# Denominator of a rational activation summed in PSUM by diagonal matmuls, with a new instruction order

## The chip, the cores and the metric

The kernel runs on one core of one Trainium2 chip. The metric is the device time of one execution in microseconds; smaller is better. The core's engines run side by side, each taking its own instructions in program order: PE (TensorE, matmuls), DVE (VectorE), ACT (ScalarE), POOL (GpSimd) and SP (here it only issues transfers). Matmuls write to PSUM, a memory of eight banks of 2 KB in each of 128 partitions; PE cannot read from it, ACT and DVE can.

## What is computed

A gated linear attention over 4 batches, 8 heads, 768 tokens and 48 columns a head, then a feed-forward block whose activation is a rational function, 384 to 2048 to 384 columns on 3072 tokens:

```python
f = 1.0 / (1.0 + np.exp(-f_logit))
for t in range(S):
    state = f[:, :, t, :, None] * state + np.einsum('bhd,bhe->bhde', k[:, :, t], v[:, :, t])
    y[:, :, t] = np.einsum('bhd,bhde->bhe', q[:, :, t], state)
...
h = x @ w_in
h2 = h * h
h3 = h2 * h
P = a[0] + a[1] * h + a[2] * h2 + a[3] * h3
Q = 1.0 + np.abs(b[0]) * np.abs(h) + np.abs(b[1]) * h2
g = P / (Q + 1e-06)
return (g @ w_out).astype(np.float32)
```

`x` is the attention's output, `a` has four numbers and `b` two.

## The kernel before

**Attention.** The 768 tokens are cut into six chunks of 128. A unit is one chunk of two batches, so there are twelve units (`NUN`), numbered by chunk and then batch pair. For a unit, `a_ef` makes log(1+exp(-f)) on ACT (an Exp and a Ln), `a_cs` sums it over the tokens by a matmul, `a_exp` takes two exponentials (tiles `A`, `Ai`), `a_mul` multiplies q and k by them on DVE into `qkp`. `a_T` transposes by sixteen matmuls into PSUM (`tp`), `a_Te` copies that to SBUF (`qkT`) on ACT. `a_sc` computes the scores of one batch in PSUM (`sc`), `a_mask` multiplies them by a triangular mask on DVE (`scm`). `a_sv` computes the new state, `a_al` the decay factor on ACT, `a_st` their product on DVE. `a_y` adds what comes from the state and from the scores (`y`), `a_ye` copies it out on ACT (`ysb`), `a_x` transposes it (`xps`) and `a_xe` copies it to `xT`, the input of the ff block, on ACT.

**Feed-forward.** The 2048 ff columns are 16 tiles of 128. A group `n` is four of them for one chunk's 512 tokens, so there are 24 groups (`NGR`), four a chunk, each on tiles of 128 x 2048 elements. `m_h` computes half a group (two ff tiles, three matmuls each) into the two banks of `hp`; `m_y` copies it to bf16 (`hy`) on ACT. On DVE, `m_q` makes z = |h|, w = (|b1| z + |b0|) z, and on ACT `m_ln` takes Ln(w + 1 + 1e-6) and `m_ex` its Exp with scale -1, the reciprocal of Q (`qi`). `m_p` builds the numerator by Horner's rule in five DVE instructions (`t`), and `m_g` multiplies it by `qi` into `gall`. `m_o` computes an output block of 128 tokens from a finished chunk with 16 matmuls, `m_oe` copies it out and SP stores it.

**Order.** The program is under a manual schedule: each engine executes its instructions in the order in which the code emits them. A prologue runs units 0, 1 and most of 2 and starts group 0. The loop then takes two groups and one attention unit per iteration `p`, while `m_o` writes out the chunk before. PSUM's eight banks are pools of one buffer each: `psA` (two banks: scores of the first batch, y), `psB` (two: cs, tp, scores of the second batch), `psh` (two: hp), `ps1` (one: state, xps) and `pso` (one: output). A buffer can be written again when its readers are done, so with one buffer for `hp` each half of a group waits for the copy of the half before. In the last chunk, whose blocks have no later groups to ride along with, `m_o` runs four tiles at a time into `psA` and `psB`.

**Loads.** SP issues in program order q, k and f of a unit (six transfers), the weights and the stores; POOL issues v and converts the weights to bf16. Staging tiles `wst` for the weights have two buffers, the inputs of a unit three.

Of the kernel before, what the change touches and what calls it, by code (L numbers as in the profile page):

```python
# [17 lines left out]
def kernel(  # L18
# [234 lines left out]
    def m_h(n, half):  # L253
        if n >= NGR:
            return
# [1 line left out]
        hp = psh.tile([P, 2, NT], F32, name="hp", tag="h")
# [59 lines left out]
    def m_o(c, b, mms=None):  # L317
        if c < 0:
            return
        if mms is None or mms[0] == 0:  # L320
            if c < NC - 1:
                ops[c, b] = pso.tile([P, DM], F32, name="op")
            else:
                pool = (psA, psB)[b // 2]
                if b % 2 == 0:
                    ops["pair", b // 2] = pool.tile([P, 2, 512], F32, name="op2", tag="AB"[b // 2])
                ops[c, b] = ops["pair", b // 2][:, b % 2, 0:DM]
        for mm in (mms or range(KF)):
# [41 lines left out]
    for g in range(1, NG):  # L370
        load_w_in(g)

    a_ef(0)
    a_cs(0)
    a_exp(0)
    a_mul(0)
# [151 lines left out]
```

## Times and profile before

| | us |
|---|---|
| median of three runs | 312.45 |
| lowest and highest run | 310.96, 314.13 |
| the profiled execution, as timed | 310.16 |
| its span, first to last instruction | 307.8 |
| DVE busy | 267.3 (87%) |
| ACT busy | 224.6 (73%) |
| PE busy with matmuls | 202.7 (66%) |
| POOL busy | 36.4 (12%) |
| mean granted clock of PE, share of full speed | 0.917 |

The profile is of one execution. A busy time is the sum over an engine's instructions, without those that only issue transfers or wait. Ends of matmuls are modelled, and overlap with the next one's start. The granted clock is 1.00 when PE runs at 2.4 GHz and 0.50 at 1.2 GHz; a value between is a mix over the stretch.

### The profile page before, as it was taken

To read this page: it belongs to the slowest core of one execution; us is meant where nothing else is said; L and a number is where in the kernel's file an instruction comes from. 1 tells how busy PE (TensorE), PEld (TensorE's weight loads), DVE (VectorE), ACT (ScalarE), POOL (GpSimd) and SP (SyncE) were. 2 spreads that over 40 slices of the span, in tenths; PEclk is the share of its full clock that TensorE was granted. 3 is DMA by queue.
4 is the path that set the end of the run, shared out by engine and by line. 5 is a ranking of instruction groups with operands and counts; after the bars stand their busy time and mean duration, and the time that the engine had idled before them with its cause. 6 is when DMAs were issued, how large, how long until landed. Compare 5 with 4: busy or idle time off the path is not lost.

```text
span 307.8 us, 4394 instructions
## 1 busy us (share of the span) xinstructions
PE 202.7 (66%) x1752; PEld 110.9 (36%) x1752; DVE 267.3 (87%) x282; ACT 224.6 (73%) x214; POOL 36.4 (12%) x42
## 2 busy tenths in 40 slices
PE   1255673653658686785984976876796758778772
PEld 0234241322324343342542533433443433334331
DVE  3253529999999999999999999999999999999981
ACT  3365477687697699698798697977996886666651
POOL 6012462036002002011020020000000000000000
PEclk9999998679689799799799899998997998999988
DMA  9999699979934009309129019000000000000002
GB/s 137 176 214 232 213 179 160 186 261 258 171 48 26 27 2 173 57 28 160 46 49 159 26 45 186 2 28 26 0 28 26 26 2 26 26 29 26 26 26 102
DMA packets 107315, 27.80 MB, mean 90 GB/s; under 512 B 100640, under 2 KB 105760, under 8 KB 107296
## 3 DMA queue, kind: packets, MB, share of 16 engines
q1 hardware_dynamic: 82336, 25.18, 40.7%
q0 software_dynamic: 24960, 2.36, 14.5%
q8 instruction: 13, 0.21, 0.3%
q14 instruction: 6, 0.05, 0.1%
HBM read 25.17 MB, written 4.72 MB: 97 GB/s over the span
## 4 chain that ended last, share of the span: by engine, by line
DVE 63%; issue 11%; DMA 9%; PE 6%; ACT 5%; SPq 5%; DVEq 0%; ACTq 0%
DVE gall L312 9%; DVE t L303 7%; DVE t L301 7%; DVE w L281 6%; DVE w L282 6%; SPq L97 5%; DVE scm L187 5%; DVE t L300 5%; DVE t L302 4%; DVE z L279 4%; DMA qn<-in_q_dram 4%; DVE qkp L128 3%; DVE t L304 3%; PE op L329 3%; DMA fn<-in_f_logit_dram 2%
## 5 line engine op out<-in xcount | busy, mean ns | idle before, releaser
L262 PE MATMUL hp<-xT,w_in_sb 128*128 128x512 bf16 x288 | 84.1, 435 | 59.3 <-ACT hy L272 57.7
L272 ACT CAST hy<-hp 128x1024 bf16<-128x1024 f32 x48 | 48.2, 1004 | 33.4 <-PE hp L262 33.4
L329 PE MATMUL op<-w_out_sb,gall 128*128 128x384 bf16 x384 | 67.9, 332 | 3.9 <-DVE gall L312 3.9
L262 PEld LDWEIGHTS <-w_in_sb 128*128 128x128 bf16 x288 | 30.3, 106 | 100.0 <-issue 79.9
L288 ACT ACTIVATE lq<-w,one_eps 128x2048 f32<-128x2048 bf16 x24 | 48.2, 2007 | 8.2 <-DVE w L282 8.1
L329 PEld LDWEIGHTS <-gall 128*128 128x128 bf16 x384 | 36.9, 99 | 29.6 <-DVE gall L312 5.3
L293 ACT ACTIVATE qi<-lq 128x2048 bf16<-128x2048 f32 x24 | 45.9, 1911 | 0.8
L187 DVE TENSOR_TENSOR scm<-sc,mask 128x1024 bf16<-128x1024 f32 x24 | 28.2, 1217 | 16.4 <-PE sc L178 16.4
L97 POOL DMA_DIRECT2D vn<-in_v_dram x24 | 22.9, 962 | 101.7 <-PE y L198 100.9
L282 DVE TENSOR_TENSOR w<-w,z 128x2048 bf16<-128x2048 bf16 x24 | 30.7, 1279 | 0.8
L312 DVE TENSOR_TENSOR gall<-t,qi 128x2048 bf16<-128x2048 bf16 x24 | 30.4, 1268 | 0.7
L303 DVE TENSOR_TENSOR t<-t,hy 128x2048 bf16<-128x2048 bf16 x24 | 29.4, 1226 | 0.8
L301 DVE TENSOR_TENSOR t<-t,hy 128x2048 bf16<-128x2048 bf16 x24 | 29.4, 1225 | 0.8
L144 ACT COPY qkT<-tp 128x2048 bf16<-128x2048 bf16 x12 | 22.4, 1866 | 2.3 <-PE tp L136 2.1
L136 PE MATMUL tp<-ident,qkp 128*128 128x128 bf16 x192 | 18.2, 265 | 7.9 <-DVE qkp L127 6.1
L136 PEld LDWEIGHTS <-qkp 128*128 128x128 bf16 x192 | 16.6, 124 | 14.1 <-DVE qkp L127 6.9
L281 DVE TENSOR_SCALAR w<-z,babs 128x2048 bf16<-128x2048 bf16 x24 | 20.1, 839 | 0.9
L300 DVE TENSOR_SCALAR t<-hy,a_sb 128x2048 bf16<-128x2048 bf16 x24 | 20.4, 851 | 0.0
L247 ACT COPY xT<-xps 128x768 bf16<-128x768 bf16 x12 | 9.6, 803 | 14.7 <-PE xps L239 14.7
L127 DVE TENSOR_TENSOR qkp<-qn,A 128x768 bf16<-128x768 f32 x12 | 11.4, 952 | 9.9 <-DMA qn<-in_q_dram 8.2
L304 DVE TENSOR_SCALAR t<-t,a_sb 128x2048 bf16<-128x2048 bf16 x24 | 18.1, 754 | 0.8
L302 DVE TENSOR_SCALAR t<-t,a_sb 128x2048 bf16<-128x2048 bf16 x24 | 18.1, 753 | 0.8
(45 smaller groups left out, 191.6 us busy)
## 6 DMA issues: line engine op xcount, KB each, us to landing
fn<-in_f_logit_dram SPq DMA_DIRECT2D x24, 192.0 KB, 5.2
kn<-in_k_dram SPq DMA_DIRECT2D x24, 192.0 KB, 5.7
qn<-in_q_dram SPq DMA_DIRECT2D x24, 192.0 KB, 5.0
out_dram<-osb SPq DMA_DIRECT2D x24, 192.0 KB, 1.9
wst<-in_moe_w_in_dram SPq DMA_DIRECT2D x4, 768.0 KB, 6.6
wst<-in_moe_w_out_dram SPq DMA_DIRECT2D x4, 768.0 KB, 5.4
vn<-in_v_dram POOLq DMA_DIRECT2D x24, 96.0 KB, 5.6
a_sb<-in_moe_a_dram SPq DMA_DIRECT2D x1, 2.0 KB, 3.7
```

Source lines behind the costliest of these rows:

```text
L97: eng.dma_start(out=dst[:, j], in_=src[u * UB + j, :, t0:t0 + C, :].rearrange("h t d -> t h d"))
L187: nc.vector.tensor_mul(m, s["sc", j].rearrange("s i p t -> s (i p) t"), mb)
L262: nc.tensor.matmul(hp[:, e, :], w_in_sb[:, kk, m * P:(m + 1) * P], xT[:, kk, :], start=(kk == 0), stop=(kk == KD - 1))
L272: nc.scalar.copy(s["y"][:, half * 2 * NT:(half + 1) * 2 * NT], s["hp", half].rearrange("p a n -> p (a n)"))
L281: nc.vector.tensor_scalar(w, z, babs[:, 1:2], babs[:, 0:1], op0=ALU.mult, op1=ALU.add)
L282: nc.vector.tensor_mul(w, w, z)
L288: nc.scalar.activation(s["lq"], s["w"], AF.Ln, bias=one_eps)
L293: nc.scalar.activation(s["qi"], s["lq"], AF.Exp, scale=-1.0)
L301: nc.vector.tensor_mul(t, t, y)
L303: nc.vector.tensor_mul(t, t, y)
L312: nc.vector.tensor_mul(galls[c][:, g * G:(g + 1) * G, :].rearrange("p a n -> p (a n)"), s["t"], s["qi"])
L329: nc.tensor.matmul(ops[c, b], galls[c][:, mm, b * C:(b + 1) * C], w_out_sb[:, mm, :], start=(mm == 0), stop=(mm == KF - 1))
```

## The change

The coefficients are rewritten so that the denominator's two are powers of two times one common factor. `coefficients` splits |b0| and |b1| into a mantissa (`bm`) and a power of two (`bp`). The weights `w_in` are multiplied by m1/m0 while POOL converts them, so h is scaled; the numerator's coefficients take the inverse powers, and the Ln of the denominator takes the factor m0*m0/m1 as its scale (`sig`). The two powers of two stand on the diagonals of two 128 x 128 bf16 matrices (`dg`). For a half group `m_u` multiplies h*h (`h2`, on DVE by `m_sq`) and |h| (`z`, by `m_abs`) by them in PE and adds both in PSUM (`u`), from which `m_ln` reads, 1024 columns at a time. h*h also serves the numerator, which is now (a3 h + a2) h2 + (a1 h + a0): `m_p1`, `m_p2`, `m_p3`. In the last chunk the groups with odd numbers keep their denominator on DVE (`m_w`, `m_lnw`).

PSUM is divided anew: a ring `psr` of two buffers of two banks takes hp, u, cs and in the prologue the second scores; `psA` takes y, tp and both scores, one after the other. The order is rewritten: the prologue has matmuls on zeros (`busy`) between its steps, the ff group's first DVE instructions are ahead of the unit's products, a step of the loop is one group, odd and even steps differ, and the denominator of a group is summed one step after its h (`gp_ = n - 1`). In the last chunk each group's output matmuls follow a step later.

```diff
-    psB = ctx.enter_context(tc.tile_pool(name="psB", bufs=1, space=PSUM))
-    psh = ctx.enter_context(tc.tile_pool(name="psh", bufs=1, space=PSUM))
+    psr = ctx.enter_context(tc.tile_pool(name="psr", bufs=2, space=PSUM))
...
-    def m_q(n):
-
-        s = mg[n]
-        z = ms.tile([P, W], BF16, name="z", bufs=1)
-        nc.vector.tensor_scalar(z.bitcast(U16), s["y"].bitcast(U16), 0x7FFF, None, op0=ALU.bitwise_and)
-        w = ms.tile([P, W], BF16, name="w", bufs=1)
-        nc.vector.tensor_scalar(w, z, babs[:, 1:2], babs[:, 0:1], op0=ALU.mult, op1=ALU.add)
-        nc.vector.tensor_mul(w, w, z)
-        s["w"] = w
...
+    def m_sq(n):
+        s = mg[n]
+        s["h2"] = ms.tile([P, W], BF16, name="h2")
+        nc.vector.tensor_mul(s["h2"], s["y"], s["y"])
+
+    def m_abs(n):
+        s = mg[n]
+        s["z"] = ms.tile([P, W], BF16, name="z")
+        nc.vector.tensor_scalar(s["z"].bitcast(U16), s["y"].bitcast(U16), 0x7FFF, None,
+                                op0=ALU.bitwise_and)
+
+    def m_u(n, half):
+
+        s = mg[n]
+        u = psr.tile([P, 2, NT], F32, name="u", tag="r")
+        for i, src in enumerate((s["h2"], s["z"])):
+            for e in range(2):
+                nc.tensor.matmul(u[:, e, :], dg[:, 1 - i, :],
+                                 src[:, (half * 2 + e) * NT:(half * 2 + e + 1) * NT],
+                                 start=(i == 0), stop=(i == 1))
+        s["u", half] = u
+
+    def m_w(n):
+
+        s = mg[n]
+        s["w"] = ms.tile([P, W], BF16, name="pb", bufs=1)
+        nc.vector.tensor_scalar(s["w"], s["z"], bp[:, 1:2], bp[:, 0:1], op0=ALU.mult, op1=ALU.add)
+        s["u"] = ms.tile([P, W], BF16, name="w", bufs=1)
+        nc.vector.tensor_mul(s["u"], s["w"], s["z"])
+
+    def m_lnw(n):
         s = mg[n]
         s["lq"] = ms.tile([P, W], F32, name="lq", bufs=1)
-        nc.scalar.activation(s["lq"], s["w"], AF.Ln, bias=one_eps)
+        nc.scalar.activation(s["lq"], s["u"], AF.Ln, scale=sig[:, 2:3], bias=1.0 + 1e-6)
+
+    def m_ln(n, half):
+        s = mg[n]
+        if half == 0:
+            s["lq"] = ms.tile([P, W], F32, name="lq", bufs=1)
+        nc.scalar.activation(s["lq"][:, half * 2 * NT:(half + 1) * 2 * NT],
+                             s["u", half].rearrange("p a n -> p (a n)"), AF.Ln,
+                             scale=sig[:, 2:3], bias=1.0 + 1e-6)
...
+    def m_p1(n):
+
+        s = mg[n]
+        s["t"] = ms.tile([P, W], BF16, name="t")
+        nc.vector.tensor_scalar(s["t"], s["y"], a_sb[:, 3:4], a_sb[:, 2:3], op0=ALU.mult, op1=ALU.add)
+        nc.vector.tensor_mul(s["t"], s["t"], s["h2"])
+
+    def m_p2(n):
+        s = mg[n]
+        s["pb"] = ms.tile([P, W], BF16, name="pb", bufs=1)
+        nc.vector.tensor_scalar(s["pb"], s["y"], a_sb[:, 1:2], a_sb[:, 0:1], op0=ALU.mult, op1=ALU.add)
+
+    def m_p3(n):
+        s = mg[n]
+        nc.vector.tensor_add(s["t"], s["t"], s["pb"])
...
-        nc.gpsimd.tensor_copy(w_in_sb[:, :, g * G * P:(g + 1) * G * P], t)
+        nc.gpsimd.tensor_scalar(w_in_sb[:, :, g * G * P:(g + 1) * G * P], t, sig[:, 0:1], None, op0=ALU.mult)
...
+    def busy(k):
+
+        for _ in range(k):
+            nc.tensor.matmul(warm, zeros[:, 0:P], zeros, start=True, stop=True)
...
+        nc.vector.reciprocal(rm, bm)
+        nc.vector.tensor_mul(sig[:, 0:1], bm[:, 1:2], rm[:, 0:1])
+        nc.vector.tensor_mul(sig[:, 1:2], bm[:, 0:1], rm[:, 1:2])
+        nc.vector.tensor_mul(sig[:, 2:3], bm[:, 0:1], sig[:, 1:2])
+        for i in range(3):
+            nc.vector.tensor_scalar(a_sb[:, 1 + i:4], a_sb[:, 1 + i:4], sig[:, 1:2], None, op0=ALU.mult)
+        for i in range(2):
+            nc.vector.tensor_scalar(dg[:, i, :], ident, bp[:, i:i + 1], None, op0=ALU.mult)
...
+    m_h(0, 0)
+    m_h(0, 1)
+    m_y(0, 0)
+    m_y(0, 1)
+    a_ef(2)
+    m_h(1, 0)
+    m_y(1, 0)
+    a_cs(2)
+    m_h(1, 1)
+    a_exp(2, 0)
+    a_exp(2, 1)
+    m_y(1, 1)
+    busy(5)
...
+    for n in range(1, NGR - NG):
+        gp_, gn, gh = n - 1, n, n + 1
+        if n % 2:
+            mu, mf = (n + 5) // 2, (n + 3) // 2
...
+    for n in range(NGR - NG, NGR):
+        g = n % NG
+        if n % 2:
+            m_w(n)
+            m_lnw(n)
...
+    for b in range(B):
+        m_o(NC - 1, b, range((NG - 1) * G, NG * G))
         m_oe(NC - 1, b, (nc.scalar, nc.vector)[b % 2])
```

What the order does is seen in the engines' instructions. On DVE, in the middle of the loop, a group that carries the masks stood so before (z, w and t are the group's tiles, `scm` the masked scores, `gall` the product with the reciprocal):

```order
L279 TENSOR_SCALAR z<-hy 128x2048
L281 TENSOR_SCALAR w<-z,babs 128x2048
L282 TENSOR_TENSOR w<-w,z 128x2048
L300 TENSOR_SCALAR t<-hy,a_sb 128x2048
L301 TENSOR_TENSOR t<-t,hy 128x2048
L302 TENSOR_SCALAR t<-t,a_sb 128x2048
L303 TENSOR_TENSOR t<-t,hy 128x2048
L304 TENSOR_SCALAR t<-t,a_sb 128x2048
L187 TENSOR_TENSOR scm_1914<-sc,mask 128x1024
L187 TENSOR_TENSOR scm_1916<-sc,mask 128x1024
L312 TENSOR_TENSOR gall<-t,qi 128x2048
```

and after the change so (`h_1752` is h*h, `pb` the linear half of the numerator):

```order
L277 TENSOR_TENSOR h_1752<-hy 128x2048
L282 TENSOR_SCALAR z<-hy 128x2048
L326 TENSOR_SCALAR t<-hy,a_sb 128x2048
L327 TENSOR_TENSOR t<-t,h_1752 128x2048
L332 TENSOR_SCALAR pb<-hy,a_sb 128x2048
L190 TENSOR_TENSOR scm_1827<-sc,mask 128x1024
L336 TENSOR_TENSOR t<-t,pb 128x2048
L190 TENSOR_TENSOR scm_1868<-sc,mask 128x1024
L343 TENSOR_TENSOR gall<-t,qi 128x2048
```

Eleven instructions become nine, the two masks are parted by an addition, and the `gall` at the end belongs to the group before, not to this one.

On ACT, in the middle of the loop, from behind the copy of the transposed q and k (`qkT`) to the two exponentials of the next unit (`A`, `Ai`), before:

```order
L288 ACTIVATE lq<-w,one_eps 128x2048
L293 ACTIVATE qi<-lq 128x2048
L272 CAST hy<-hp 128x1024
L106 ACTIVATE ef<-fn 128x768
L107 ACTIVATE lsp_105<-ef 128x16x48
L339 COPY osb<-op 128x384
L272 CAST hy<-hp 128x1024
L223 ACTIVATE alast<-sv 128x8
L214 CAST ysb<-y 128x2x8x48
L122 ACTIVATE A<-cs 128x768
L122 ACTIVATE Ai<-cs 128x768
```

and now (`A_1883` and `A_1924` are those two exponentials):

```order
L368 COPY osb<-op 128x384
L313 ACTIVATE lq<-u,sig 128x1024 x2
L226 ACTIVATE alast<-sv 128x8
L320 ACTIVATE qi<-lq 128x2048
L271 CAST hy<-hp 128x1024
L110 ACTIVATE ef<-fn 128x768
L111 ACTIVATE lsp_101<-ef 128x16x48
L271 CAST hy<-hp 128x1024
L368 COPY osb<-op 128x384
L124 ACTIVATE A_1883<-cs 128x768
L217 CAST ysb<-y 128x2x8x48
L124 ACTIVATE A_1924<-cs 128x768
```

The Ln is two instructions that wait for PE, and the copy of y has moved between the two exponentials.

On DVE at the end of the prologue, the first ff group stood behind the masks of unit 2 before:

```order
L127 TENSOR_TENSOR qkp_102<-qn,A 128x2x8x48
L128 TENSOR_TENSOR qkp_102<-kn,Ai 128x2x8x48
L187 TENSOR_TENSOR scm_525<-sc,mask 128x1024
L187 TENSOR_TENSOR scm_527<-sc,mask 128x1024
L279 TENSOR_SCALAR z<-hy 128x2048
```

and now stands ahead of the products of that unit:

```order
L277 TENSOR_TENSOR h_531<-hy 128x2048
L282 TENSOR_SCALAR z<-hy 128x2048
L326 TENSOR_SCALAR t<-hy,a_sb 128x2048
L327 TENSOR_TENSOR t<-t,h_531 128x2048
L332 TENSOR_SCALAR pb<-hy,a_sb 128x2048
L130 TENSOR_TENSOR qkp_99<-qn,A_503 128x2x8x48
L131 TENSOR_TENSOR qkp_99<-kn,A_505 128x2x8x48
L336 TENSOR_TENSOR t<-t,pb 128x2048
L277 TENSOR_TENSOR h_583<-hy 128x2048
```

The masks of unit 2 come later, after the first instructions of group 1.

## Rows read from the trace of the kernel before

**Rows 1.** Windows: length; busy PE, PEld, DVE, ACT, POOL; clock; DMA share, GB/s

```profile
0.00:46.24 46.24, 22.30 (x261) 14.04 (x261) 18.67 (x20) 24.00 (x29) 16.52 (x24) 1.00 1.29 192
46.24:69.18 22.94, 12.04 (x105) 6.05 (x107) 22.52 (x24) 16.96 (x15) 5.01 (x4) 0.78 1.19 202
...
148.25:170.28 22.03, 16.61 (x152) 9.38 (x151) 21.61 (x25) 18.54 (x18) 1.84 (x2) 0.89 0.54 82
170.28:264.02 93.74, 69.18 (x592) 37.39 (x590) 91.63 (x99) 77.22 (x71) 2.24 (x2) 0.94 0.18 34
264.02:299.50 35.48, 27.24 (x144) 14.13 (x141) 34.14 (x36) 23.01 (x18) 0.00 (x0) 0.95 0.07 27
299.50:307.80 8.30, 2.77 (x16) 1.48 (x16) 1.11 (x2) 0.96 (x2) 0.00 (x0) 0.82 0.27 100
```

**Rows 2.** Waits: who waited for whom, us in total, times, longest

```profile
PE hp L262 <- ACT hy L272: 57.7, 33, 5.6
```

**Rows 3.** Timeline: start, us, engine, line; in brackets the idle time before

```profile
35.38 2.72 PE L262 MATMUL hp<-xT,w_in_sb 128*128 128x512 bf16 x6 [1.28 <-ACT xT L247]
...
43.97 2.36 DVE L187 TENSOR_TENSOR scm<-sc,mask 128x1024 bf16<-128x1024 f32 x2 [6.91 <-PE sc L178]
...
46.24 0.68 DVE L279 TENSOR_SCALAR z<-hy 128x2048 uint16<-128x2048 uint16 x1
```

**Rows 4.** Groups by line on DVE: busy us, mean ns, idle before

```profile
L282 DVE TENSOR_TENSOR w<-w,z 128x2048 bf16<-128x2048 bf16 x24 | 30.7, 1279 | 0.8
...
L301 DVE TENSOR_TENSOR t<-t,hy 128x2048 bf16<-128x2048 bf16 x24 | 29.4, 1225 | 0.8
...
L300 DVE TENSOR_SCALAR t<-hy,a_sb 128x2048 bf16<-128x2048 bf16 x24 | 20.4, 851 | 0.0
L281 DVE TENSOR_SCALAR w<-z,babs 128x2048 bf16<-128x2048 bf16 x24 | 20.1, 839 | 0.9
...
L302 DVE TENSOR_SCALAR t<-t,a_sb 128x2048 bf16<-128x2048 bf16 x24 | 18.1, 753 | 0.8
```

**Rows 5.** Groups by line on ACT: the ff block's copy, Ln and Exp

```profile
L272 ACT CAST hy<-hp 128x1024 bf16<-128x1024 f32 x48 | 48.2, 1004 | 33.4 <-PE hp L262 33.4
L288 ACT ACTIVATE lq<-w,one_eps 128x2048 f32<-128x2048 bf16 x24 | 48.2, 2007 | 8.2 <-DVE w L282 8.1
L293 ACT ACTIVATE qi<-lq 128x2048 bf16<-128x2048 f32 x24 | 45.9, 1911 | 0.8
```

**Rows 6.** Timeline of PE in the pair from 148.25 us and behind it

```profile
148.40 1.91 PE L136 MATMUL tp<-ident,qkp 128*128 128x128 bf16 x16
...
150.10 2.01 PE L262 MATMUL hp<-xT,w_in_sb 128*128 128x512 bf16 x6
...
157.01 1.46 PE L262 MATMUL hp<-xT,w_in_sb 128*128 128x512 bf16 x6 [0.58 <-ACT hy L272]
...
168.85 2.72 PE L262 MATMUL hp<-xT,w_in_sb 128*128 128x512 bf16 x6 [3.03 <-ACT hy L272]
...
171.37 1.22 PE L136 MATMUL tp<-ident,qkp 128*128 128x128 bf16 x16
```

**Rows 7.** Timeline of the attention's steps in the same pair

```profile
158.40 0.37 PE L198 MATMUL y<-state,qkT 48*128 48x48 bf16 x16
...
158.70 0.58 PE L198 MATMUL y<-vn,scm 128*128 128x48 bf16 x16
...
159.12 0.49 PE L113 MATMUL cs<-lsp,U 128*128 128x384 bf16 x2
...
159.81 0.81 ACT L214 CAST ysb<-y 128x768 bf16<-128x768 f32 x1
...
160.50 0.84 ACT L122 ACTIVATE A<-cs 128x768 f32<-128x768 f32 x1
...
168.27 0.95 DVE L128 TENSOR_TENSOR qkp<-kn,Ai 128x768 bf16<-128x768 f32 x1
```

**Rows 8.** Timeline behind the last `gall`: a copy of the output blocks

```profile
303.50 0.48 ACT L339 COPY osb<-op 128x384 f32<-128x384 f32 x1 [2.00 <-DMA out_dram<-osb]
```

More of the change, by code (lines that the diff above doesn't have):

```diff
@@ L170, in a_sv, with a_sc @@
                                      start=False, stop=True, skip_group_check=True)
-    def a_sc(n, j):
+    def a_sc(n, j, ring=False):
         s = at_[n]
-        sc = (psA, psB)[j].tile([C, 2, HP, C], F32, name="sc", tag="AB"[j])
+        sc = (psr if ring else psA).tile([C, 2, HP, C], F32, name="sc", tag="r" if ring else "A")
         for p in range(HP):
@@ L253, in m_h @@
     def m_h(n, half):
[L254 to L255 removed]
         c, g = divmod(n, NG)
[L257 removed]
+        hp = psr.tile([P, 2, NT], F32, name="hp", tag="r")
         xT = xTs[c].rearrange("p k b t -> p k (b t)")
@@ L315, with m_o @@
     ops = {}
[L317 to L321, printed above, removed]
+    def m_o(c, b, mms):
+        if mms[0] == 0:
+            if c < NC - 1 or b == 3:
                 ops[c, b] = pso.tile([P, DM], F32, name="op")
-            else:
[L324 to L328, printed above, removed]
+            elif b == 2:
+                ops[c, b] = ps1.tile([P, 512], F32, name="opl", tag="w1")[:, 0:DM]
+            else:
+                if b == 0:
+                    ops["pair"] = psA.tile([P, 2, 512], F32, name="op2", tag="A")
+                ops[c, b] = ops["pair"][:, b, 0:DM]
+        for mm in mms:
             nc.tensor.matmul(ops[c, b], galls[c][:, mm, b * C:(b + 1) * C], w_out_sb[:, mm, :],
@@ new lines, in isg, with isu, o_of, oe_of @@
+    def isg(n):
+        return 0 <= n < NGR
+    def isu(m):
+        return 0 <= m < NUN
+    def o_of(n, part):
+        c, b = (n - 1) // NG - 1, (n - 1) % NG
+        half = KF // 2
+        if 0 <= c < NC - 1:
+            m_o(c, b, range(part * half, (part + 1) * half))
+    def oe_of(n):
+        c, b = (n - 1) // NG - 1, (n - 1) % NG
+        if 0 <= c < NC - 1:
+            m_oe(c, b)
+    busy(12)
+    a_ef(0)
+    a_cs(0)
+    a_exp(0, 0)
+    a_exp(0, 1)
+    a_mul(0)
+    coefficients()
@@ L368 @@
     load_w_in(0)
     load(2)
[L370 to L376, printed above, removed]
+    load_w_in(1)
+    busy(14)
     a_T(0)
+    busy(6)
     a_ef(1)
-    a_cs(1, psh)
     a_Te(0)
     a_sc(0, 0)
-    a_sc(0, 1)
+    a_sc(0, 1, ring=True)
+    a_cs(1)
+    a_exp(1, 0)
+    a_exp(1, 1)
     a_sv(0)
-    a_exp(1)
+    busy(3)
+    a_al(0)
     a_mask(0, 0)
     a_mask(0, 1)
-    a_al(0)
     a_y(0)
+    busy(6)
+    a_ye(0)
     a_mul(1)
-    a_ye(0)
@@ L393 @@
     a_x(0)
+    busy(6)
+    a_Te(1)
     a_xe(0)
-    a_Te(1)
-    load(3)
-    nc.scalar.activation(babs, b_sb, AF.Abs)
     a_sc(1, 0)
-    a_sc(1, 1)
+    a_sc(1, 1, ring=True)
     a_sv(1)
-    a_ef(2)
+    busy(5)
+    a_al(1)
     a_mask(1, 0)
     a_mask(1, 1)
-    a_al(1)
     a_y(1)
-    a_cs(2)
+    busy(4)
     a_ye(1)
@@ new lines @@
+    n = NGR - NG
+    m_sq(n)
+    m_abs(n)
+    m_u(n - 1, 0)
+    m_ln(n - 1, 0)
+    m_u(n - 1, 1)
+    m_ln(n - 1, 1)
+    m_h(n + 1, 0)
+    m_ex(n - 1)
+    m_y(n + 1, 0)
+    m_h(n + 1, 1)
+    m_y(n + 1, 1)
+    o_of(n, 0)
+    o_of(n, 1)
+    oe_of(n)
+    m_p1(n)
+    m_p2(n)
+    m_p3(n)
+    m_g(n - 1)
+    for n in range(NGR - NG, NGR):
[3 more added lines that the diff above has]
+            m_lnw(n)
+        else:
+            m_u(n, 0)
+            m_ln(n, 0)
+            m_u(n, 1)
+            m_ln(n, 1)
+        if n + 2 < NGR:
+            m_h(n + 2, 0)
+            m_h(n + 2, 1)
+        m_ex(n)
+        if n + 2 < NGR:
+            m_y(n + 2, 0)
+            m_y(n + 2, 1)
+        if n > NGR - NG:
+            m_p1(n)
+            m_p2(n)
+            m_p3(n)
+            m_g(n - 1)
+        if n + 1 < NGR:
+            m_sq(n + 1)
+            m_abs(n + 1)
+        o_of(n + 1, 0)
+        o_of(n + 1, 1)
+        oe_of(n + 1)
+        if g > 0:
+            for b in range(3):
+                m_o(NC - 1, b, range((g - 1) * G, g * G))
```

256 lines of the change are left out of this document (147 added, 109 removed).

## The prediction

> **What bounds the kernel now.** I read the busy times by stretch first, cutting the span where the first DVE instruction of every second group of four ff tiles starts (call two such groups and the attention unit that rides along a pair). After a head of 46.24 us a pair takes 22.03 us, and in it DVE is busy 21.61, ACT 18.54 and PE 16.61 [rows 1]. The nine pairs from 69.18 to 264.02 take 194.84 us, 21.65 each; the last four groups, which carry no attention, take 35.48 of which DVE fills 34.14; 8.30 follow [rows 1]. So from 46 us on DVE is the bound, and the other two wait for it: all 57.7 us that the first ff matmuls lose to ACT's copies (line 262, one PSUM slot `hp`) are slack while DVE is full [rows 2]. In the head DVE is idle: it waits 6.91 us for the scores of unit 2 and starts its first ff instruction at 46.24, although the first matmuls of ff group 0 began at 35.38 [rows 3].
>
> **What the change takes from DVE.** Per group it removes the affine for w (0.839), its product with z (1.279), one of the two products by y (1.225) and two additions of a constant (0.753 each): 4.85 us. It adds h*h, p3's addition of two bf16 tiles (both of the kind of line 301: 1.225) and one affine (line 300's kind, 0.851): 3.30 us [rows 4]. The abs, one affine, one product and the product into `gall` stay. Net 1.55 us a group, 3.10 a pair: DVE needs 21.61 - 3.10 = 18.5 us of a pair.
>
> **What it puts on ACT.** The Ln of 2048 columns (2.007) becomes two of 1024 from PSUM. No Ln from PSUM of this width is in the trace. The nearest row is the copy of 1024 columns out of PSUM, 1.004 [rows 5]. The Ln with its bias from a tile takes 0.096 more than the Exp of the same width without one (2.007 against 1.911), and the new Ln takes its scale from a tile, so 1.10 each. Two are 2.20, +0.19 a group; bounds 0 (two at 1.004) and +0.4. ACT's pair goes from 18.54 to 18.9.
>
> **What it puts on PE.** Eight matmuls of 128x512 a group. Six of that shape take 1.46 us where the clock is high [rows 6], so four take 0.97 and the eight 1.95; 3.9 a pair. PE's 16.61 in the pair from 148.25 holds slow stretches: six ff matmuls in 2.01 instead of 1.46, sixteen transposes in 1.91 instead of 1.22 [rows 6]; without these 1.2 it is 15.4. Sum 19.3 us a pair at the high clock. The three engines then stand at 18.5, 18.9 and 19.3: the bound passes from DVE to PE, and none has room.
>
> **Where the new order makes them wait.** Ring `psr` has two slots for hp, u, cs and some sc. In an odd step the second half of u takes the slot of cs, which is free when both exponentials have read it: cs 0.49, A 0.84, the copy of y 0.81, the other exponential 0.84 make 2.98 us from the start of cs; PE has cs 0.49, y 0.37 + 0.58 and the first half of u 0.97 to do meanwhile, 2.4 [rows 7]. It loses 0.6 there, once a pair: 19.3 becomes 19.9. Against that the modelled ends of successive matmuls overlap, so the true PE work is somewhat less than 19.3. The pair has 18.5 as its lowest value (DVE alone) and 21.7 as its highest (PE at the granted clock of 0.89 that the pair from 148.25 had [rows 1]: 19.3 / 0.89). I take 19.4, between ACT's sum and PE's with the wait, because the waits of each of these engines are filled by its next work only in part. Nine pairs are 174.6; the last has no unit to prepare and the first three steps no output matmuls, which I put at -3 together (two exponentials and half a us per step). 171.6 against 194.84: **-23.2**.
>
> **The head.** Loads, their queue order up to unit 2 and the chain through units 0 and 1 stay, but a and b now go ahead of unit 1 on SP, and the coefficients are made on DVE while it waits for scores. The `busy` matmuls stand in front of PE's own work, but where PE waits; zero, with +-1.5 as bounds. So the ff matmuls again start at 35.4. Two halves at 1.46 (the first ran in 2.72 [rows 3]) and a copy of 1.0 [rows 5] bring DVE to its first ff instruction at 39.2 instead of 46.24. From there to the first instruction of group 2, DVE has two groups without the second `gall` (2 x 6.1 + 1.27), two pairs of masks and products by A: two masks 2.36 [rows 3], four products at 0.95 [rows 7] and one state, about 20 us: 59.3 at the earliest. It will be later. In step 1 the second scores of unit 2 go through the ring behind both Ln, and the transposes, ff matmuls and copies for group 2 (1.22 + 2.92 + 1.0 = 5.1) come behind the products of unit 3, covered only by an addition and a `gall` (2.5). I take 64, between 59.3 and the old 69.18: **-5**.
>
> **The end.** In the last four groups two of the denominators stay on DVE (w and its product, 2.1 each): 34.14 - 4 x 1.55 + 4.2 = 32.1. PE has 27.24 [rows 1] and three groups' u more, 5.9: 33.1, and it waits for copies early in that stretch, when each u stands behind output matmuls. Bounds 32.1 and 38; I take 36, **+0.5**. Behind it, output block 1 shares its tile with block 0 and its matmuls now wait for block 0's copy, but block 0 no longer waits for the matmuls of block 1; the later blocks wait for an output buffer, as the copy at 303.50 did for 2.00 us [rows 8]: **+0.2**.
>
> **Sum.** 307.8 - 5 - 23.2 + 0.5 + 0.2 = 280.3 of span; the profiled execution took 310.16 for a span of 307.8, so 282.7 for a run. The median of the runs is 2.3 above that execution, within their own spread of 3.2, so I leave it at 283.
>
> **The rivals.**
>
> *Forecast: the bound passes to PE and ACT, pair 18.9 to 20.4.* 275 to 292 us. Chance 0.58.
>
> *Everything fits: DVE stays the bound.* If the u matmuls hide completely, a pair takes 18.5 (9 x 0.9 = 8.1 less) and step 1 does not stall (4.7 less): 270. For it: before, DVE was busy 21.61 of 22.03 although every engine takes its work in a fixed order [rows 1]. Against it: PE had 5 us of slack in a pair then and would have less than none now. Chance 0.22.
>
> *PE's clock stays where it is now.* The granted clock was 0.89 in the pair from 148.25, 0.94 over 170 to 264, but 0.78 in the pair from 46.24, where PE was busy 12.04 of 22.94 [rows 1]; before the stretch of 2.72 instead of 1.46 PE had been idle 3.03 [rows 6]. At 0.89 the pair is 21.7, 9 x 2.3 = 20.7 more: 304. Against it: the row with more work (69.18 of 93.74) has the higher clock, and the change fills the idle time. The Trainium skill (TensorE: Matmul & The Clock Gate, "A second HAM failure mode: psum-queue depth-cycling") tells of a kernel whose matmuls of 512 columns cycle through PSUM banks, so that short idle times between groups keep the clock going up and down. That is this case, with two slots for u and hp; by that rule the pair is the 21.7 above, by the trend of the rows 19.4. Chance 0.12.
>
> *PE at low clock makes it slower.* The same mechanism, further down: at the 0.78 of the pair from 46.24 a pair is 19.3 / 0.78 = 24.7, 48 more: 331. It decides from the point where a pair costs 3.3 more than forecast, 22.7, a granted clock of 0.85. For it: ff matmuls, u, scores and masks now depend on each other through two slots and one slot `psA`, so a wait on ACT stops PE. Against it: a pair at 22.7 would leave PE waiting 3 us in it, in pieces, less than it waits now. Chance 0.05.
>
> *The change gives back what it takes.* Waits at the ring of 3.3 us a pair at full clock, with the two slots held through ACT's long Exp: 312. Chance 0.03, because a slot is held by u 0.97 + 1.10, and by hp 1.46 + 1.91 + 1.00, twice each in some 19 us.
>
> **Chances.** About 1% is what a measurement of this kernel can tell from no change. Faster 0.58 + 0.22 + 0.12 = 0.92, within 1% 0.03, slower 0.05. The range leaves out the slow cases and half of the clock case: 269 to 297; the likeliest case's own is 275 to 292.
>
> **What would show it.** DVE's busy time should fall by about 33 us (24 groups at 1.55, less 4.2 for the two denominators that stay) to 234, ACT's stay within 10 of 225, PE's rise by 30 or more beyond its warming matmuls, with a granted clock of 0.95 or more between 70 and 235 us. The Ln of 1024 columns should take 1.0 to 1.15. Group 2's h*h should start at 60 to 67, and from there a pair should repeat every 19 to 20 us, with DVE idle about 1 us in it and PE idle less than 1.5. The prediction is wrong if the pair repeats above 20.5 or below 18.5, if PE shows stretches of six matmuls in 2.7 us in the loop, if u waits for a slot longer than 1 us, or if the loads, now queued behind outputs on SP in another order, are what the exponentials or the products wait for.

## The result and the profile after

The changed kernel takes 284.8 us, median of four runs (283.51 to 286.58), beside 311.7 us for the kernel before in the same session: a ratio of 0.917 with a 95% interval of 0.908 to 0.926, so 8% faster. Forecast were 283 us with a range of 269 to 297. The profiled execution has a span of 283.2 us, 24.6 less than the 307.8 of before.

The stretches of the changed kernel, cut at the same instructions as [rows 1]: the first DVE instruction of ff group 0, of group 2, and of group 20, and the end of the last `gall`. The columns are start and end, length, then busy time of PE, PEld, DVE, ACT and POOL with counts, granted clock, DMA share, GB/s.

```profile
0.00:35.30 35.30, 27.37 (x231) 13.95 (x231) 13.85 (x27) 16.70 (x20) 15.75 (x18) 0.95 1.15 185
35.30:67.92 32.62, 19.22 (x156) 10.69 (x157) 28.13 (x20) 17.40 (x20) 22.48 (x11) 0.79 1.13 219
67.92:237.12 169.20, 152.77 (x1393) 82.33 (x1393) 161.09 (x167) 163.20 (x170) 13.65 (x15) 0.99 0.50 72
...
162.23:181.63 19.40, 18.67 (x175) 10.31 (x173) 18.18 (x19) 18.68 (x21) 1.75 (x2) 1.00 0.63 92
...
237.12:271.51 34.39, 32.80 (x181) 17.42 (x179) 32.60 (x33) 27.73 (x25) 0.00 (x0) 1.00 0.08 30
271.51:283.20 11.69, 5.72 (x35) 3.13 (x32) 1.12 (x3) 0.96 (x2) 0.00 (x0) 0.86 0.23 83
```

Read against [rows 1], group 2 starts at 67.92 instead of 69.18, so the head gives 1.3 us. The nine pairs take 169.20 instead of 194.84, which is 25.6 less and more than the whole gain. What follows takes 34.39 + 11.69 = 46.08 instead of 35.48 + 8.30 = 43.78, 2.3 more. In a steady pair, 162.23 to 181.63, the three engines are busy 18.67, 18.18 and 18.68 us of 19.40: PE and ACT share the bound, DVE follows half a microsecond behind. The clock, 0.89 and 0.94 in the stretches of the loop in [rows 1], is 0.99 over all nine pairs.

Groups by line (busy time, mean ns of one, idle time ahead of them): the operations that are new or changed.

```profile
L313 ACT ACTIVATE lq<-u,sig 128x1024 f32<-128x1024 f32 x44 | 47.8, 1125 | 5.4 <-PE u L291 4.5
L271 ACT CAST hy<-hp 128x1024 bf16<-128x1024 f32 x48 | 47.5, 1007 | 5.1 <-PE hp L263 4.5
...
L277 DVE TENSOR_TENSOR h<-hy 128x2048 bf16<-128x2048 bf16 x24 | 29.7, 1239 | 14.6 <-ACT hy L271 14.5
...
L375 POOL TENSOR_SCALAR w_in_sb<-wst,sig 128x1536 bf16<-128x1536 f32 x4 | 19.1, 4773 | 18.3 <-DMA wst<-in_moe_w_in_dram 18.3
```

The Ln of 1024 columns from PSUM takes 1.125 us, the copy of the same width 1.007. The last line is the one that the prediction had not priced: POOL's conversion of `w_in` now multiplies, and takes 4.77 us each. In the kernel before the same tiles were converted without a factor:

```profile
L346 POOL CAST w_in_sb<-wst 128x1536 bf16<-128x1536 f32 x4 | 6.2, 1548 | 25.6 <-DMA wst<-in_moe_w_in_dram 25.6
```

What that does in the head is seen in the timeline of the changed kernel (start, us, engine, line; in brackets the idle time before):

```profile
31.48 4.15 POOL L375 TENSOR_SCALAR w_in_sb<-wst,sig 128x1536 bf16<-128x1536 f32 x1 [2.66 <-DMA wst<-in_moe_w_in_dram]
...
35.30 1.23 DVE L277 TENSOR_TENSOR h<-hy 128x2048 bf16<-128x2048 bf16 x1 [6.14 <-ACT hy L271]
...
35.63 5.44 POOL L375 TENSOR_SCALAR w_in_sb<-wst,sig 128x1536 bf16<-128x1536 f32 x1
...
37.04 4.57 DVE L326 TENSOR_SCALAR t<-hy,a_sb 128x2048 bf16<-128x2048 bf16 x1
...
41.06 4.58 POOL L375 TENSOR_SCALAR w_in_sb<-wst,sig 128x1536 bf16<-128x1536 f32 x1
...
41.65 4.18 DVE L327 TENSOR_TENSOR t<-t,h 128x2048 bf16<-128x2048 bf16 x1
45.76 0.80 DVE L332 TENSOR_SCALAR pb<-hy,a_sb 128x2048 bf16<-128x2048 bf16 x1
...
49.85 1.87 ACT L147 COPY qkT<-tp 128x2048 bf16<-128x2048 bf16 x1 [9.09 <-PE tp L139]
...
67.92 1.63 DVE L277 TENSOR_TENSOR h<-hy 128x2048 bf16<-128x2048 bf16 x1 [2.90 <-ACT hy L271]
```

Three conversions fill POOL from 31.48 to 45.64. Beside them DVE's affine (0.85 on average before [rows 4]) takes 4.57 and its product (1.225) 4.18. That is 6.7 us more than the two take elsewhere. The unit's products stand behind them on DVE, and the transposes behind the products; ACT waits 9.09 for these. PE also waits 1.47 us for a converted tile, ahead of group 1's first half, but that group's copies end at 40.76, long before DVE takes them at 49.36.

### The profile page after: what moved, and what is told of

It is laid out like the page before. It is cut to its first block, busy times and chain, and to the rows that moved or that the text cites. A ratio compares the mean times of both kernels' runs of the same rounds, so it can differ in the third digit from the quotient of the medians.

```text
span 283.2 us, 4853 instructions
## 1 busy us (share of the span) xinstructions
PE 237.9 (84%) x1992; PEld 127.5 (45%) x1992; DVE 236.8 (84%) x249; ACT 226.0 (80%) x235; POOL 51.9 (18%) x42
## 4 chain that ended last, share of the span: by engine, by line
PE 37%; DVE 21%; ACT 17%; issue 9%; SPq 8%; DMA 5%; POOL 1%; ACTq 0%; DVEq 0%
PE hp L263 14%; PE op L360 12%; SPq L101 8%; PE u L291 7%; ACT hy L271 4%; ACT lq L313 4%; DVE h L277 3%; DVE t L327 3%; DMA wst<-in_moe_w_in_dram 2%; DVE t L326 2%; ACT A L124 2%; DMA fn<-in_f_logit_dram 2%; PE tp L139 2%; DVE pb L332 2%; DVE t L336 2%
## 5 line engine op out<-in xcount | busy, mean ns | idle before, releaser
L263 PE MATMUL hp<-xT,w_in_sb 128*128 128x512 bf16 x288 | 67.1, 382 | 7.3 <-ACT xT L250 4.0
L313 ACT ACTIVATE lq<-u,sig 128x1024 f32<-128x1024 f32 x44 | 47.8, 1125 | 5.4 <-PE u L291 4.5
L277 DVE TENSOR_TENSOR h<-hy 128x2048 bf16<-128x2048 bf16 x24 | 29.7, 1239 | 14.6 <-ACT hy L271 14.5
L101 POOL DMA_DIRECT2D vn<-in_v_dram x24 | 22.7, 951 | 94.8 <-PE y L201 94.0
L327 DVE TENSOR_TENSOR t<-t,h 128x2048 bf16<-128x2048 bf16 x24 | 33.5, 1396 | 0.8
L291 PE MATMUL u<-h,dg 128*128 128x512 bf16 x88 | 27.4, 394 | 6.1 <-ACT A L124 5.6
L336 DVE TENSOR_TENSOR t<-t,pb 128x2048 bf16<-128x2048 bf16 x24 | 29.3, 1220 | 0.5
L291 PE MATMUL u<-z,dg 128*128 128x512 bf16 x88 | 27.4, 395 | 0.0
L375 POOL TENSOR_SCALAR w_in_sb<-wst,sig 128x1536 bf16<-128x1536 f32 x4 | 19.1, 4773 | 18.3 <-DMA wst<-in_moe_w_in_dram 18.3
L124 ACT ACTIVATE A<-cs 128x768 f32<-128x768 f32 x24 | 19.3, 818 | 1.7 <-PE cs L117 1.7
L332 DVE TENSOR_SCALAR pb<-hy,a_sb 128x2048 bf16<-128x2048 bf16 x24 | 19.8, 824 | 0.0
```

Source lines behind the costliest of these rows:

```text
L101: eng.dma_start(out=dst[:, j], in_=src[u * UB + j, :, t0:t0 + C, :].rearrange("h t d -> t h d"))
L263: nc.tensor.matmul(hp[:, e, :], w_in_sb[:, kk, m * P:(m + 1) * P], xT[:, kk, :], start=(kk == 0), stop=(kk == KD - 1))
L277: nc.vector.tensor_mul(s["h2"], s["y"], s["y"])
L291: nc.tensor.matmul(u[:, e, :], dg[:, 1 - i, :], src[:, (half * 2 + e) * NT:(half * 2 + e + 1) * NT], start=(i == 0), stop=(i == 1))
L313: nc.scalar.activation(s["lq"][:, half * 2 * NT:(half + 1) * 2 * NT], s["u", half].rearrange("p a n -> p (a n)"), AF.Ln, scale=sig[:, 2:3] ...
L327: nc.vector.tensor_mul(s["t"], s["t"], s["h2"])
```

## The experiments

**One part undone: the factor off POOL.** The conversion is a plain copy again, and the factor goes into the scale of ACT's copy of `xT`.

```diff
-        nc.gpsimd.tensor_scalar(w_in_sb[:, :, g * G * P:(g + 1) * G * P], t, sig[:, 0:1], None, op0=ALU.mult)
+        nc.gpsimd.tensor_copy(w_in_sb[:, :, g * G * P:(g + 1) * G * P], t)
...
-        nc.scalar.copy(xTs[c][:, :, u * UB:(u + 1) * UB, :].rearrange("p k b t -> p b k t"), s["xps"])
+        nc.scalar.activation(xTs[c][:, :, u * UB:(u + 1) * UB, :].rearrange("p k b t -> p b k t"), s["xps"],
+                             AF.Copy, scale=sig[:, 0:1])
```

> The changed kernel with one edit: POOL converts w_in as the kernel before did (a plain cast), and the factor m1/m0 is applied by ACT in the twelve copies to xT. Theory: in the changed kernel POOL's scaling conversion takes 4.77 us instead of 1.55, and while three of them run (31.5 to 45.6 us) DVE's first affine and product take 4.57 and 4.18 us instead of 0.8 and 1.2. Then here the conversions take 1.5 to 2.2 us, those two DVE instructions 0.8 to 2.3, group 2 starts at 61 to 63 us instead of 67.9, and the time falls by 4 to 6.5 us, to 278 to 281. Rival: any conversion beside DVE costs DVE the same, or the head waits for weights and loads anyway; then group 2 starts at 66 to 68 and the time stays at 283 to 286.

Measured: 281.8 us, ratio 0.906 (0.903 to 0.909); span 279.7, 3.5 less than the changed kernel. Timeline of the same place:

```profile
37.64 1.88 POOL L376 CAST w_in_sb<-wst 128x1536 bf16<-128x1536 f32 x1 [2.33 <-DMA wst<-in_moe_w_in_dram]
38.11 1.96 DVE L327 TENSOR_SCALAR t<-hy,a_sb 128x2048 bf16<-128x2048 bf16 x1
...
40.10 1.23 DVE L328 TENSOR_TENSOR t<-t,h 128x2048 bf16<-128x2048 bf16 x1
...
63.66 2.02 DVE L278 TENSOR_TENSOR h<-hy 128x2048 bf16<-128x2048 bf16 x1 [3.48 <-ACT hy L272]
```

The conversions are back at 1.65 on average, the product is back at 1.23, and the affine, which now meets one short conversion, takes 1.96. Group 2 starts 4.3 us earlier. Group 2 and the time both just miss what was expected (61 to 63, 278 to 281). The loop pays part of the gain back: it takes 170.26 instead of 169.20, with ACT copying `xT` in 895 ns instead of 794. Nine such copies are 0.9 us, which fits a loop that loses what ACT loses; a shorter ACT was not tried.

```profile
63.66:233.92 170.26, 154.15 (x1393) 82.84 (x1393) 161.57 (x167) 164.07 (x170) 13.89 (x15) 0.98 0.49 72
L250 ACT ACTIVATE xT<-xps,sig 128x768 bf16<-128x768 bf16 x12 | 10.7, 895 | 0.8 <-PE xps L242 0.8
```

**Is it the factor's tile or the operation?** The multiplication stays on POOL, with a constant 1.0 in place of the factor from a tile.

```diff
-        nc.gpsimd.tensor_scalar(w_in_sb[:, :, g * G * P:(g + 1) * G * P], t, sig[:, 0:1], None, op0=ALU.mult)
+        nc.gpsimd.tensor_scalar(w_in_sb[:, :, g * G * P:(g + 1) * G * P], t, 1.0, None, op0=ALU.mult)
```

> The changed kernel with POOL's conversion of w_in still a tensor_scalar, but with the constant 1.0 in the instruction instead of the per-partition factor (h is not scaled, so the output is slightly another function). It tells which part of the new instruction costs the time. If the per-partition operand: 1.5 to 1.9 us each, as the cast, and group 2 starts at 61 to 63. If the form: 4.1 to 5 us each, as now, and group 2 at 67 to 69.

Measured: 285.25 us in a single run, span 282.9. The group by line, and group 2 in the timeline:

```profile
L375 POOL TENSOR_SCALAR w_in_sb<-wst 128x1536 bf16<-128x1536 f32 x4 | 17.4, 4363 | 18.1 <-DMA wst<-in_moe_w_in_dram 18.1
...
67.99 1.23 DVE L277 TENSOR_TENSOR h<-hy 128x2048 bf16<-128x2048 bf16 x1 [2.69 <-ACT hy L271]
```

With a constant it takes 4.36 us, and group 2 starts where it did. So it is the operation on POOL, not its operand. The 0.4 between 4.36 and 4.77 tells nothing: with the factor from a tile the mean is 4.30 to 4.84 in the other traces.

**One part undone: the matmuls on zeros.**

```diff
-        for _ in range(k):
+        for _ in range(0):
             nc.tensor.matmul(warm, zeros[:, 0:P], zeros, start=True, stop=True)
```

> The changed kernel without its 64 matmuls on zeros. Theory (the prediction's): they stand where PE waits, and what they give is a higher clock in the prologue, worth about half a microsecond for each of the transposes, scores and first ff matmuls of units 0 and 1; group 0 then starts 1 to 2.5 us later than 35.3, the conversions on POOL hide most of it, and the time rises by 0 to 2 us. Rival: they delay the attention's steps in the prologue; group 0 starts 1 us earlier or more and the time falls. Second rival: without them the clock stays low far into the loop, the granted clock from 67.9 to 86.6 us falls from 1.00 to below 0.9 and the time rises by 4 us or more.

Measured: 286.05 us, ratio 0.920 (0.916 to 0.923), not to be told from the changed kernel; span 283.3. Timeline:

```profile
38.79 1.24 DVE L277 TENSOR_TENSOR h<-hy 128x2048 bf16<-128x2048 bf16 x1 [8.70 <-ACT hy L271]
...
68.01 1.23 DVE L277 TENSOR_TENSOR h<-hy 128x2048 bf16<-128x2048 bf16 x1 [0.64 <-ACT hy L271]
```

With them group 0 starts 3.5 us earlier (35.30), but group 2 at 67.92 instead of 68.01: the lead is gone by then. The loop behind it takes 169.15 us at clock 0.99, as with them, so they are not what holds the clock there. As the changed kernel stands they are worth nothing; without the slow conversions they were not tested.

A second trace of the changed kernel (the run beside the combined kernel, below) shows where the lead goes:

```profile
20.90 4.95 POOL L375 TENSOR_SCALAR w_in_sb<-wst,sig 128x1536 bf16<-128x1536 f32 x1 [14.43 <-DMA wst<-in_moe_w_in_dram]
...
21.82 3.97 DVE L131 TENSOR_TENSOR qkp<-kn,A 128x768 bf16<-128x768 f32 x1
...
38.94 1.23 DVE L277 TENSOR_TENSOR h<-hy 128x2048 bf16<-128x2048 bf16 x1 [6.14 <-ACT hy L271]
...
40.11 4.68 POOL L375 TENSOR_SCALAR w_in_sb<-wst,sig 128x1536 bf16<-128x1536 f32 x1 [0.45 <-DMA wst<-in_moe_w_in_dram]
...
40.68 4.65 DVE L326 TENSOR_SCALAR t<-hy,a_sb 128x2048 bf16<-128x2048 bf16 x1
...
68.16 1.22 DVE L277 TENSOR_TENSOR h<-hy 128x2048 bf16<-128x2048 bf16 x1 [1.92 <-ACT hy L271]
```

Here the first conversion already stretches a product of unit 1 on DVE (3.97, where the first trace has 0.95), and group 0 starts at 38.94 although the matmuls on zeros are there. Group 2 is again at 68.16. So a start of group 0 some 3.5 us earlier or later, be it by the matmuls on zeros or by that product, does not move group 2 by more than 0.3: in all three traces DVE gets through its first product with h*h only when POOL's last conversion has ended, at 45.83, 46.59 and 46.75 us.

**The wait for the slot of `cs` taken away.** In the odd steps both exponentials go ahead of the copy of y, so that `cs` leaves its ring slot earlier.

```diff
                 a_exp(mu, 0)
+                a_exp(mu, 1)
...
-            if isu(mu):
+            if isu(mu) and n == 1:
                 a_exp(mu, 1)
```

> The changed kernel with ACT's two exponentials of the next unit one behind the other at the start of an odd step, ahead of the copy of y, instead of around it. Theory (the prediction's wait): the second half of u waits once a pair (0.7 to 1.1 us) for the slot of cs, which the second exponential frees; without the copy in between (0.8) that wait goes, PE is the bound, and a pair falls from 19.2 towards ACT's 18.7: 0.4 to 0.7 a pair, 4 to 6 us in all, 279 to 281. Rival: the copy of y now ends later, so x, the transposes and the ff matmuls of the next group start later by as much, and the time stays within 1 us of 284.8.

Measured: 283.65 us, ratio 0.912 (0.909 to 0.915), span 281.8, 1.4 less. In the changed kernel the waits over five pairs (104.75 to 200.65; waiting line, line waited for, us, times, longest) hold this one, and the chain of waits shows it pair by pair:

```profile
PE u L291 <- ACT A L124: 3.7, 5, 0.7
...
114.36 0.48 ACT osb L368
114.84 0.71 ACT A L124
115.55 0.74 ACT ysb L217
116.29 0.72 ACT A L124
...
117.06 1.04 PE u L291 x4
```

In the experiment that wait is gone, and two of its pairs read:

```profile
123.51:142.64 19.13, 18.75 (x174) 10.26 (x172) 18.19 (x19) 18.52 (x21) 1.75 (x2) 1.00 0.62 94
142.64:161.46 18.82, 17.85 (x168) 9.70 (x166) 18.19 (x21) 18.52 (x21) 1.75 (x2) 1.00 0.65 97
```

Five pairs take 94.81 us instead of 95.90, 0.22 less each, where the wait was 0.73; over the nine pairs it is 1.7 us (167.52 instead of 169.20). So the expected 4 to 6 us did not come. PE is busy 18.75 of the 19.13 us of the one pair, ACT 18.52 of the 18.82 of the other: both stay at the bound. The gain in time is small against the noise: the interval of the ratio overlaps that of the changed kernel, 0.914 to 0.920 when it was run again.

**Less work on PE.** The |h| term of the denominator is left out, and with it half of the matmuls for u.

```diff
-        for i, src in enumerate((s["h2"], s["z"])):
+        for i, src in enumerate((s["h2"],)):
...
-                                 start=(i == 0), stop=(i == 1))
+                                 start=True, stop=True)
```

> The changed kernel with half of the matmuls with dg: only h*h goes into the denominator, the term in |h| is left out (z is still made), so its output is another function. PE loses 0.87 us a group. Theory: PE is the bound of the loop (18.7 of 19.4 us busy in a pair), so a pair falls from 19.2 until ACT (18.7) stops it: 0.4 to 0.6 a pair, with the last groups 5 to 7 us, 278 to 280. Rival: ACT, also 18.7 busy, is the bound: less than 2 us.

Measured: 282.9 us, ratio 0.907 (0.902 to 0.912). The changed kernel, run again, has 0.917 (0.914 to 0.920), so this is about 1% faster. Of the 1.3 us that the profiled execution's span is shorter, 1.2 come before group 2 (66.75 instead of 67.92). Its nine pairs take 169.42 us: no gain there from 8 fewer matmuls a pair. Two pairs of it, and the timeline in the second:

```profile
123.75:142.35 18.60, 16.95 (x166) 9.45 (x164) 18.00 (x21) 18.57 (x21) 2.03 (x2) 1.00 0.67 101
142.35:161.92 19.57, 17.73 (x160) 9.77 (x159) 18.09 (x20) 18.30 (x21) 2.23 (x2) 0.91 0.66 97
...
154.17 0.59 PE L291 MATMUL u<-h,dg 128*128 128x512 bf16 x2 [1.42 <-ACT A L124]
...
156.96 3.88 PE L263 MATMUL hp<-xT,w_in_sb 128*128 128x512 bf16 x12
```

Where the clock holds, the pair is ACT's sum, 18.57 of 18.60. In the other pair PE waits 1.42 us for the slot (0.73 in the changed kernel), the next twelve ff matmuls take 3.88 us instead of 2.75, part of them at the lower of the clock's two levels (1.2 and 2.4 GHz; the granted clock of the pair is 0.91), and the pair is longer than that of the changed kernel. That the wait brought the clock down is not shown: the pair before has a wait of 1.22 at a clock of 1.00. So relieving PE alone brings little, and in this execution's loop nothing, for two reasons: ACT is the bound at once, as the rival said, and the clock no longer stays up all the time.

**The new order alone.** Every denominator is made on DVE in the way that the changed kernel keeps for two groups of the last chunk, with the one Ln of 2048 columns; no matmuls for u. The order of the rest stays.

```diff
     def m_u(n, half):

+        if half == 0:
+            m_w(n)
+        return
...
     def m_ln(n, half):
+        if half == 0:
+            m_lnw(n)
+        return
```

> The changed kernel with every denominator on DVE, as its last chunk's odd groups have it: the affine of z and the product with z (2.05 us a group) and one Ln of 2048 columns, no matmul with dg; h*h, the order and the ring stay. Theory: the gain is DVE's, the order alone gives little: a pair needs 18.2 + 4.1 = 22.3 us of DVE, nine pairs 28 us more than the changed kernel's 169, the last groups 4 more: 312 to 318, about the kernel before. Rival: the new order brings a third of the gain or more by itself (waits outside DVE): 300 or less.

Measured: 336.23 us, ratio 1.079 (1.074 to 1.085), far above what was expected. A pair of it, the nine pairs, and the timeline in that pair:

```profile
143.72:167.64 23.92, 17.40 (x155) 9.86 (x153) 22.24 (x23) 18.50 (x19) 2.33 (x2) 0.86 0.51 75
...
71.42:285.05 213.63, 149.89 (x1251) 81.51 (x1252) 197.06 (x204) 162.09 (x152) 13.51 (x12) 0.82 0.35 53
...
159.60 0.80 PE L242 MATMUL xps<-ident,ysb 128*128 128x128 bf16 x6 [3.93 <-DVE state L234]
...
162.59 3.97 PE L263 MATMUL hp<-xT,w_in_sb 128*128 128x512 bf16 x12
...
167.64 1.23 DVE L277 TENSOR_TENSOR h<-hy 128x2048 bf16<-128x2048 bf16 x1 [1.25 <-ACT hy L271]
```

DVE's 22.24 us in the pair are near its 21.61 of before [rows 1], but the pair takes 23.92 instead of 22.03. In this order PE waits for DVE's state (3.93), runs the next twelve ff matmuls in 3.97 us, and DVE then waits for their copy. So with the denominator on DVE this order brings no gain, and waits and a lower clock make it worse than the old one. In this order the gain in the loop is there only with the sum in PSUM. The other half, the sum in PSUM under the old order, was not run, nor another place in the new order for the two instructions on DVE; what sum and order are worth apart stays open.

**The end.** The twelve early matmuls of output block 3 go directly ahead of its other four, behind the last `gall` and the blocks 0 to 2.

```diff
-    m_o(NC - 1, 3, range((NG - 1) * G))
     m_g(n)
     for b in range(B):
+        if b == 3:
+            m_o(NC - 1, 3, range((NG - 1) * G))
```

> The changed kernel with the twelve early matmuls of the last output block moved from ahead of the last blocks' matmuls to directly before that block's own. Theory: at the end PE is behind (last product into gall ends at 271.5, first output copy starts at 275.2); with 2.0 us less ahead of block 0 the first copy starts at about 273.1 and the end comes 1.5 to 2 us earlier, 283. Rival: the end is set by the two output buffers that wait for their stores (2.0 each); then the copies of blocks 2 and 3 start when they do now, and the end moves by less than 0.5 us.

Measured: 283.82 us, ratio 0.913 (0.910 to 0.917); span 281.7. The end in the timeline of the changed kernel:

```profile
272.36 2.76 PE L360 MATMUL op<-w_out_sb,gall 128*128 128x384 bf16 x16
275.16 0.48 ACT L368 COPY osb<-op 128x384 f32<-128x384 f32 x1 [4.53 <-PE op L360]
...
279.15 0.56 DVE L366 COPY osb<-op 128x384 f32<-128x384 f32 x1 [2.00 <-DMA out_dram<-osb]
```

and in the experiment:

```profile
272.98 0.48 ACT L368 COPY osb<-op 128x384 f32<-128x384 f32 x1 [2.59 <-PE op L360]
```

In the changed kernel block 0's four last matmuls stand behind twelve of block 3, and its copy starts only at 275.16. With the twelve moved it starts 2.2 us earlier, and the span is 1.5 shorter, as expected, 1.3 of it behind the last `gall`. By the times alone it would not be told from noise, since the interval overlaps that of the changed kernel (0.914 to 0.920).

**All three together.** The plain conversion, the exponentials first and the moved matmuls (the three diffs above), and beside it the changed kernel once more.

> The changed kernel with three edits together: the plain cast of w_in with the factor in the copies to xT, both exponentials ahead of the copy of y, and the last block's early matmuls behind the other blocks. Alone they took 3.5, 1.4 and 1.5 us off the span. They lie in the prologue, the loop and the end, so they should add up: span 276 to 278, runs 277.5 to 279.5. If ACT's longer copies to xT (0.1 us, twelve of them) meet an ACT that has lost its waits, the loop's gain goes and the span is 278 to 279.

> The changed kernel as it is, once more, beside the combined one and the kernel before on one chip: 283 to 286.5, ratio 0.91 to 0.92.

Measured: 278.94 us, ratio 0.896 (0.894 to 0.898), where the changed kernel has 285.64 us and 0.917 (0.914 to 0.920): 2.3% faster than it, and the fastest version here. Its span of 276.4 is 6.8 less than that of the changed kernel, where the three alone gave 3.5, 1.4 and 1.5. Its nine pairs and its end:

```profile
63.97:231.96 167.99, 152.93 (x1393) 82.01 (x1393) 160.74 (x167) 162.81 (x170) 12.37 (x14) 1.00 0.49 72
231.96:276.40 44.44, 38.52 (x214) 20.54 (x211) 33.68 (x35) 28.66 (x27) 0.00 (x0) 1.00 0.12 45
```

## Where the prediction was right and where not

The time, 284.8, lies 1.8 above the 283 and inside the range. The terms were right for the loop; those of the head and of the tail were too good by 3.7 and 3.2 us, and a loop better by 2.4 and last groups better by 1.6 made up for 4.0 of these 6.9. That the total comes so near is in part luck.

- **DVE's part.** 18.5 us a pair was forecast, 18.18 measured; 234 in all, 236.8 measured, with some 7 us of it the two stretched instructions of the head (4.57 and 4.18 in place of 0.85 and 1.225). Nothing failed here.
- **ACT's part.** The Ln at 1.10 measured 1.125; 18.9 a pair measured 18.68.
- **PE's part and the pair.** 19.3 was forecast, 18.67 measured in the pair from 162.23, at least in part for the reason that the text gave (the ends of successive matmuls overlap): leaving out half of the matmuls for u took 1.72 us off PE's pair (18.67 to 16.95), so all of them are some 3.4, not 3.9. The wait for the slot of `cs`, forecast at 0.6, is 0.73 in the steady pairs and 1.08 at its longest; above 1 us the text had called itself wrong, and the pair did not suffer for it. PE's busy time rose by 35.2, of which the matmuls on zeros are 18.6, so by less than the 30 forecast beyond them: u cost less, and the ff matmuls with `w_in` fell from 84.1 to 67.1. The pair was taken as 19.4; five pairs of 95.90 us are 19.18 each. That the bound moves off DVE and lies with PE and ACT together is what three experiments bear out: with less work on PE a pair ended at ACT's 18.57 of 18.60, with the wait taken away both engines were near full, and with 0.1 us more in each copy of `xT` on ACT the loop got 1.06 longer. So "everything fits" was no case, though near.
- **The clock.** The rival with a granted clock of 0.89 did not come: 0.99 over the nine pairs. The Trainium skill (TensorE: Matmul & The Clock Gate, "A second HAM failure mode: psum-queue depth-cycling") tells of matmuls of 512 columns that cycle through PSUM banks and of a clock that goes up and down with the short idle times between them. The trace of the changed kernel does not show that, with matmuls of 512 columns through two slots and 0.73 us of waiting in a steady pair. A lower clock does come where PE has less work or longer waits: the experiment with half of u has a pair at 0.91 and the one with the denominator on DVE pairs at 0.86, with ff matmuls in 3.9 us instead of 2.75. The latter has a pair of 23.92, beyond the 22.7 of the slow case, but not by PE at low clock alone: DVE is busy 22.24 of it, PE 17.40.
- **The head.** This step failed. Forecast were -5 and group 2 at 64; measured -1.3 and 67.92. Group 0 was forecast at 39.2 and started at 35.30 in the one trace and at 38.94 in the other; group 2 was late in both. The step listed what DVE, PE and ACT do and left out POOL's conversion, which the diff shows as a new operation; it was costed at nothing without a row, so the path through DVE behind it was missed. The experiment without it has group 2 at 63.66, about the 64 of the forecast. That the slow conversions stretch DVE's instructions is shown by their end times too: the affine that started at 37.04 ended at 41.61, just behind the conversion that ended at 35.63 + 5.44 = 41.07, and the product at 45.83, behind the next one's 45.64. In the second trace the affine ends 0.54 behind its conversion as well (45.33 and 44.79), and without the matmuls on zeros it is the abs that takes 4.57 and ends 0.55 behind (44.52 and 43.97). The Trainium skill (SBUF — State Buffer, "Who interferes with whom") states that DVE and GpSimd share one pair of ports, and that of two instructions that need it the one that issues first holds it until it ends, while the other is blocked. The ends of the affines and the abs agree with that; the product, which takes 1.2 alone, ended only 0.19 behind the conversion, so not all of it fits a full block. That it is this port was not tested by itself.
- **The matmuls on zeros.** Priced at zero with bounds of 1.5; group 2 moved by 0.1 without them, with a span of 283.3.
- **The end.** The last four groups were forecast at 36 and took 34.39; DVE's 32.60 and PE's 32.80 there were forecast at 32.1 and 33.1, so the waits assumed between them were too many. The tail was forecast at +0.2 and is +3.4 (11.69 against 8.30 [rows 1]). The step looked at the tiles of the output and at [rows 8], not at PE's queue, in which twelve matmuls of block 3 are ahead of block 0's; moving them took 1.3 of it back. The rest was not followed further.

## What to carry to other kernels

When a change relieves the bound engine, sum the other engines' work in the same stretch first: here 3.4 us taken from DVE gave 2.6 in a steady pair (22.03 to 19.40), because PE and ACT then stand at the top, and relieving PE alone after that gave 0.2 a pair or nothing. Price every operation that changes its kind, on the idle engines too: a conversion on POOL that becomes a multiplication took three times as long and reached the path through DVE. An order written for one balance of the engines can lose in another, so test it apart from the arithmetic that it came with, both ways round: here only one of the two was done.

## What was not expected of the hardware

- On POOL, a `tensor_scalar` from f32 to bf16 of 128x1536 takes 4.77 us (4.30 to 4.84 in the mean of each trace) with its factor from a tile and 4.36 with a constant, where a cast of the same tile takes 1.55 to 1.65.
- DVE's bf16 instructions get longer beside it: an affine of 128x2048 from 0.81 to 4.57, a product from 1.22 to 4.18, an abs from 0.69 to 4.57. Which one is hit differs from trace to trace. A plain cast of POOL stretches the affine to 1.96.
- PE with fewer matmuls got a lower clock: 1323 records in the nine pairs at 0.95 instead of 1393 at 0.99, in the same 169 us.
- A copy on ACT of 128x768 with its scale from a tile takes 895 ns, without one 794.
